# A dense layer's odd chunk of 96 hidden units, made with 128 columns of weights, on one Trainium2 core

## The chip, the cores and the metric

The kernel runs on one core of one Trainium2 chip. The metric is the device time of one execution in microseconds (us); of the kernel before there are three runs, and their median is used. TensorE (PE) multiplies a stationary operand, loaded by a weight load (PEld in the profile), with a moving operand that streams past it; results go to PSUM. VectorE (DVE), ScalarE (ACT) and GpSimd (POOL) work on SBUF and PSUM beside it; SyncE (SP) issues most transfers. Each engine runs its own instructions in order and waits on semaphores for the others.

## The reference, cut to what matters

Two kinds of layer alternate: attention (A), dense (B), attention, dense. Both layers of a kind share their weights.

```python
def _B_ref(x, w1, w2):               # x 2048 x 512, w1 512 x 1376, w2 1376 x 512
    h = jnp.einsum('bsd,df->bsf', x, w1)
    h = jnp.maximum(h, zero)
    return jnp.einsum('bsf,fd->bsd', h, w2)

x = x + _A_ref(_layernorm(x), A_mem0, Wq, Wk, Wv, Wo, seg_len)
x = x + _B_ref(_layernorm(x), w1, w2)
x = x + _A_ref(...)
x = x + _B_ref(...)
```

`_A_ref` goes through the 2,048 tokens in 64 segments of 32. Each segment attends, with 32 heads of 128, to itself and to 8 memory rows, and the first 8 rows of its output are the next segment's memory, so the segments form a recurrence. The dense layer maps each token on its own: 512 values to 1,376 hidden units, ReLU, and back to 512. The order of the hidden units doesn't matter, so long as the columns of `w1` and the rows of `w2` agree.

## The kernel before

**Steps.** One loop runs over `k`. Step `k` holds segment `k` of the first attention layer and segment `k - 4` of the second, so that the two recurrences run beside each other; at the start and at the end only one of them is there (a "single" step: k = 1 to 3 and 64 to 67). A step makes queries and keys for half of the heads (`qk(0)`, line 575), scores and softmax for them, then `qk(1)`, `scores` (line 609) and `softmax` of the other half, then `transpose_p` (line 656), `weighted_v` (line 682), the output projection of the memory rows (line 617), the new memory (line 820) and values (lines 346, 765).

**The dense layer.** Step `k` also does the dense layer for the rows that were finished two steps earlier, `d = k - 2`: normally 64 rows (32 from each of the two chains), sometimes 32. `dense_h` makes the hidden units, transposed: a chunk of hidden units lies on the partitions of PSUM, the rows lie along the free axis. 1,376 is 10 times 128 and 96 more, so there are `NFC = 11` chunks, and `F_LAST = 96`. For each chunk four matmuls run, one for each 128 of the 512 inputs; the stationary operand is a block of `w1` (128 inputs by the chunk's units) and the moving one the 64 (or 32) rows. So every matmul of line 507 has a weight load of its own. The chunks are made in two pieces: chunks 8 to 10 first, then 0 to 7 (three pieces in the last call: 8 to 10, 0 to 3, 4 to 7). A piece has one PSUM tile `hp`, of a pool of two buffers (`ps_fill`) that other stages use too. ReLU takes a piece from PSUM to `hT` in SBUF: the full chunks of a piece in one ACT instruction (line 513), the chunk of 96 units in another (line 515); in the last call chunks 4 to 7 go through DVE (line 511). `dense_y` (line 528) multiplies `hT` with `w2`; for the chunk of 96 units it uses 96 partitions of both. In all there are 67 passes through the dense layer; the last one has its own second half at line 1057, which takes the chunks in the order 8, 9, 10, 0 to 7.

**Where `dense_h` stands in a step.** The order of PE, DVE, SP and POOL is the order of the program, with calls under `tc.high_priority` and the rest written out by hand in `step`. In a normal step all 44 matmuls of `dense_h` come after `qk(1)` and before the second `scores`. In every fourth step up to k = 37 (`split(k)`: k = 5, 9, ... 37) and only there, the piece of chunks 8 to 10 stands there alone, and the other piece comes after the scores. In a single step `dense_h` comes after the second softmax. ACT is the one engine whose order isn't written out: a planner sorts its instructions by priority and by when it reckons that they are ready.

**What DVE does next to it.** `scores` adds into a PSUM tile in which DVE has put the mask (line 601), one tile for each of the two layers; the copies of the keys (line 583) and the softmax (lines 625, 629, 641, 642, 646) are DVE's too, the exponential (line 631) and the copies of the queries (line 581) ACT's.

Of the kernel before, what the change touches and what calls it, by code (L numbers as in the profile page):

```python
# [10 lines left out]
ACTF = mybir.ActivationFunctionType  # L11
# [11 lines left out]
def kernel(  # L23
# [14 lines left out]
    nc = tc.nc  # L38
# [4 lines left out]
    Dff = B_w1.shape[1]  # L43
# [7 lines left out]
    NFC = (Dff + 127) // 128  # L51
    F_LAST = Dff - (NFC - 1) * 128
# [43 lines left out]
    def span(d):  # L96
        offs = ([0] if has0(d) else []) + [o for o, _ in slots_of.get(d, [])]
        return base(d) + min(offs), base(d) + max(offs) + 32
# [52 lines left out]
    w1_sb = const.tile([128, NC4, Dff], BF)  # L151
    w2_sb = const.tile([128, NFC, Dm], BF)
# [3 lines left out]
    def load_dense():  # L156
        nc.sync.dma_start(out=w1_sb[:], in_=B_w1.rearrange("(c p) f -> p c f", p=128))
        nc.sync.dma_start(out=w2_sb[:, 0:NFC - 1, :],
                          in_=B_w2[0:(NFC - 1) * 128, :].rearrange("(c p) d -> p c d", p=128))
        nc.sync.dma_start(out=w2_sb[0:F_LAST, NFC - 1, :], in_=B_w2[(NFC - 1) * 128:Dff, :])  # L160

    mhalf_t = const.tile([128, 1], F32)
    nc.vector.memset(mhalf_t[:], -0.5)
# [322 lines left out]

    def dense_h(d, parts=slice(None)):
        if not 0 <= d <= LAST:  # L490
            return
        lo, hi = span(d)
        n = hi - lo

        def cols(c4):
            return xnT_tiles[d + 2][:, c4, lo:hi]

        if not parts.start:
            hT_tiles[d] = wk.tile([128, NFC, 64], BF, tag="hT", bufs=1, name="hT")
        hT = hT_tiles[d]  # L500
        pieces = ((8, NFC), (0, 4), (4, 8)) if d == LAST - 1 else ((8, NFC), (0, 8))
        for f0, f1 in pieces[parts]:
            hp = ps_fill.tile([128, 8, 64], F32, tag="fill", name="hp")
            for fc in range(f0, f1):
                fs = 128 if fc < NFC - 1 else F_LAST
                for c4 in range(NC4):
                    nc.tensor.matmul(hp[0:fs, fc - f0, 0:n], lhsT=w1_sb[:, c4, fc * 128:fc * 128 + fs],  # L507
                                     rhs=cols(c4), start=(c4 == 0), stop=(c4 == NC4 - 1))
            nfull = min(f1, NFC - 1) - f0
            if (f0, f1) == (4, 8):  # L510
                nc.vector.tensor_scalar_max(out=hT[:, f0:f1, 0:n], in0=hp[:, 0:nfull, 0:n], scalar1=0.0)
            else:
                nc.scalar.activation(out=hT[:, f0:f0 + nfull, 0:n], in_=hp[:, 0:nfull, 0:n], func=ACTF.Relu)
            if f1 == NFC:
                nc.scalar.activation(out=hT[0:F_LAST, NFC - 1, 0:n], in_=hp[0:F_LAST, nfull, 0:n], func=ACTF.Relu)

    def dense_y(d, f0, f1, bank=1):
        if not 0 <= d <= LAST:
# [376 lines left out]
    def step(k):  # L895
# [30 lines left out]
        def probabilities():  # L926

            softmax(0, act, by_pe, ess)
            if not by_pe:
                turn_p()  # L930
            if k % 4 == 3 and has_x:
                inputs_T(n_x)
            if has0(k + 1):
                load_x(k + 1)
            if k == 1:
                load_dense()
# [3 lines left out]
        if single:  # L940
            block(k, part, mid)
        elif light:
            dense_h(k - 2, slice(0, 1))
            block(k, part, 16)
        else:
            dense_h(k - 2)
# [3 lines left out]
        if single:  # L950
            dense_h(k - 2, slice(0, 1) if k == LAST else slice(None))
            block(k, mid, H)
            if k == LAST:
                keep_busy(3)
        elif light:
            dense_h(k - 2, slice(1, None))
            block(k, 16, H)
        else:
            block(k, part, H)
# [56 lines left out]
    with tc.manual_schedule(engines={mybir.EngineType.PE, mybir.EngineType.DVE, mybir.EngineType.SP,  # L1016
# [25 lines left out]
        d = LAST - 1  # L1042
# [10 lines left out]
        for fc in order:  # L1053
            fs = 128 if fc < NFC - 1 else F_LAST
            for q in range(4):
                u, j = divmod(q, 2)
# [45 lines left out]
```

## Time and profile before

| what | value |
|---|---|
| device time, median of 3 runs | 1598.08 us (1596.8 to 1599.88) |
| the profiled execution: its own time / its span | 1596.61 us / 1594.8 us |
| PE busy | 1565.9 us (98%), 42,680 matmuls |
| weight loads busy | 1320.7 us (83%) |
| DVE / ACT / POOL busy | 1268.4 (80%) / 738.9 (46%) / 349.8 us (22%) |
| clock granted to TensorE | 1.0 |
| line 507, PE busy (64 and 32 rows, 128 and 96 units) | 102.2 us, 2,948 matmuls |
| ReLU of full chunks, line 513 | 134 instructions, 35.8 + 17.0 + 2.7 + 1.3 us |
| ReLU of the chunk of 96 units, line 515 | 67 instructions, 12.9 + 1.1 us |

A profile page lists busy time by engine, then a chain of work followed back from the last instruction to what released it, then groups of instructions. In a group's row, `out<-in` names the tiles, `128*96` is the size of the stationary operand (inputs by columns), `128x64` the moving one or the tile, `xN` the count; after the bar stand the busy time, the mean duration of one in ns, and the idle time of the engine ahead of them. Durations of matmuls and weight loads overlap: what a stream of them costs is the distance from one start to the next, and that is read from the chain (a piece of the chain has its start, its length and the number of instructions in it) or from the starts of single instructions in the trace. "PE busy" therefore doesn't show by itself how fast PE goes.

### The profile page before, as it was taken

The page shows a single profiled execution, that of the slowest core. Times are in us where ns is not written, and L with a number is a line of the kernel's source. Part 1 is how long each engine was busy: PE and PEld are TensorE (multiplying, and loading weights), DVE is VectorE, ACT ScalarE, POOL GpSimd, SP SyncE. Part 2 cuts the span into 40 slices and gives each one's busy share as a digit, 9 for nine tenths or more (in the row PEclk, how much of TensorE's full clock was granted, in tenths as well). Part 3 has the DMA queues.
Part 4 walks back from the last instruction along what each step waited for, and adds up shares of the span by engine and source line. Part 5 has one row for each costly group of instructions (what it writes and reads, how often), then busy time and mean ns, then how long its engine had stood idle before and what let it go on. Part 6 is the DMA issues. An engine that isn't in the chain of part 4 may idle for free.

```text
span 1594.8 us, 94682 instructions
## 1 busy us (share of the span) xinstructions
PE 1565.9 (98%) x42680; PEld 1320.7 (83%) x42680; DVE 1268.4 (80%) x3115; ACT 738.9 (46%) x1799; POOL 349.8 (22%) x670
## 2 busy tenths in 40 slices
PE   6999999999999999999999999999999999999998
PEld 4677888888898888889888888988888898898886
DVE  4578888888888888888888888888878888887866
ACT  3434444444544544454454545445454544545433
POOL 2012222222222222222222222222222222222110
PEclk9999999999999999999999999999999999999999
DMA  9733343343343534444334443343443333233332
GB/s 369 237 78 74 76 87 89 65 98 86 77 78 83 94 64 95 84 73 87 83 87 71 98 83 77 84 83 82 80 98 79 74 88 79 78 77 93 70 75 41
DMA packets 222564, 146.38 MB, mean 92 GB/s; under 512 B 124008, under 2 KB 216528, under 8 KB 222160
## 3 DMA queue, kind: packets, MB, share of 16 engines
q1 hardware_dynamic: 218992, 136.09, 37.6%
q8 instruction: 335, 5.49, 1.5%
q0 software_dynamic: 3072, 4.20, 1.1%
q14 instruction: 69, 0.57, 0.1%
q10 hardware_dynamic: 96, 0.03, 0.0%
HBM read 65.41 MB, written 45.35 MB: 69 GB/s over the span
## 4 chain that ended last, share of the span: by engine, by line
PE 96%; DMA 2%; DVE 1%; SPq 1%; issue 0%; ACT 0%; POOL 0%; POOLq 0%; ACTq 0%
PE qp L575 38%; PE wox L365 10%; PE wo L617 8%; PE vm L765 7%; PE v L346 7%; PE hp L507 6%; PE sp L528 5%; PE pv L682 4%; PE sp L609 4%; PE vp L306 3%; DMA Wv_sb<-in_A_Wv_dram 2%; PE tp L656 1%; PE xp L478 1%; PE wox L388 1%; SPq L134 0%; PE mt L820 0%
## 5 line engine op out<-in xcount | busy, mean ns | idle before, releaser
L581 ACT CAST QT<-qp 128x480 bf16<-128x480 f32 (+3 forms) x408 | 201.7, 494 | 392.3 <-PE qp L575 392.2
L575 PE MATMUL qp<-HT,Wq_sb 128*128 128x80 bf16 (+1 forms) x8704 | 370.2, 200 | 2.1 <-POOL HT L754 1.2
L575 PE MATMUL qp<-HT,Wk_sb 128*128 128x80 bf16 (+1 forms) x8704 | 369.2, 199 | 1.5 <-DMA Wk_sb<-in_A_Wk_dram 0.7
L575 PEld LDWEIGHTS <-Wq_sb 128*128 128x128 bf16 x8704 | 325.6, 100 | 33.8 <-issue 26.5
L575 PEld LDWEIGHTS <-Wk_sb 128*128 128x128 bf16 x8704 | 328.2, 100 | 2.3 <-DMA Wk_sb<-in_A_Wk_dram 1.2
L583 DVE CAST KT<-qp 128x480 bf16<-128x480 f32 (+3 forms) x408 | 231.4, 568 | 124.0 <-PE qp L575 118.1
L646 POOL TENSOR_TENSOR P_sb<-es,sm 128x320 bf16<-128x320 f32 x185 | 130.9, 721 | 751.7 <-ACT es L631 502.2
L365 PE MATMUL wox<-Wo_sb,OTx 128*64 128x256 bf16 x2880 | 173.6, 273 | 0.0
L625 DVE TENSOR_REDUCE mx<-sp 128x8 f32<-128x320 f32 x256 | 115.0, 487 | 73.6 <-PE sp L609 72.7
L365 PEld LDWEIGHTS <-OTx 128*64 128x64 bf16 x2880 | 150.2, 110 | 2.9
L631 ACT ACTIVATE es<-es 128x320 f32<-128x320 f32 x256 | 110.7, 469 | 58.2 <-DVE es L629 57.2
L765 PE MATMUL vm<-Wv_sb,HTm 128*32 128x512 bf16 x2176 | 136.4, 380 | 0.6 <-DVE HT L834 0.6
L641 DVE TENSOR_REDUCE sm<-es 128x8 f32<-128x320 f32 x256 | 118.3, 462 | 15.0 <-ACT es L631 4.7
L617 PE MATMUL wo<-Wo_sb,OTm 128*32 128x512 bf16 x2144 | 128.9, 380 | 0.2 <-issue 0.2
L346 PE MATMUL v<-Wv_sb,xnT 128*32 128x512 bf16 x2048 | 129.0, 378 | 0.0
L601 DVE CAST sp<-maskb 128x320 f32<-128x320 bf16 x256 | 118.4, 484 | 0.0
L629 DVE TENSOR_TENSOR es<-sp,mx 128x320 f32<-128x320 f32 x256 | 113.8, 483 | 1.5
L765 PEld LDWEIGHTS <-HTm 128*32 128x32 bf16 x2176 | 90.6, 96 | 27.4 <-issue 12.3
L528 PE MATMUL sp<-w_sb,hT 128*64 128x256 bf16 (+4 forms) x1452 | 104.1, 275 | 0.2 <-issue 0.2
L769 ACT CAST VmS<-vm 128x512 bf16<-128x512 f32 x134 | 78.6, 587 | 53.8 <-PE vm L765 53.8
L507 PE MATMUL hp<-xnT,w_sb 128*128 128x64 bf16 (+3 forms) x2948 | 102.2, 193 | 0.5 <-DVE xnT L436 0.4
L507 PEld LDWEIGHTS <-w_sb 128*128 128x128 bf16 (+1 forms) x2948 | 95.1, 101 | 1.3 <-issue 0.7
(124 smaller groups left out, 2028.8 us busy)
## 6 DMA issues: line engine op xcount, KB each, us to landing
Vs<-vd SPq DMA_DIRECT2D x96, 256.0 KB
vd<-vst SPq DMA_DIRECT2D x181, 128.0 KB
vmd<-VmS SPq DMA_DIRECT2D x134, 128.0 KB
Vs<-vmd SPq DMA_DIRECT2D x254, 32.0 KB
Vs<-vmd SPq DMA_DIRECT2D x60, 128.0 KB
Wq_sb<-in_A_Wq_dram SPq DMA_DIRECT2D x2, 2048.0 KB
Wk_sb<-in_A_Wk_dram SPq DMA_DIRECT2D x2, 2048.0 KB
Wv_sb<-in_A_Wv_dram SPq DMA_DIRECT2D x2, 2048.0 KB
```

Of the source, the lines that this page charges most:

```text
L346: nc.tensor.matmul(vp[32 * j:32 * j + 32, :], lhsT=tokens[:, c4, :], rhs=Wv_sb[:, c4, n * 512:(n + 1) * 512], start=(c4 == 0), stop=(c4 == ...
L365: nc.tensor.matmul(out[64 * j:64 * j + nr, 0:256], lhsT=lhsT, rhs=rhs[:, 256 * j:256 * j + 256], start=start, stop=stop, tile_position=(0, ...
L507: nc.tensor.matmul(hp[0:fs, fc - f0, 0:n], lhsT=w1_sb[:, c4, fc * 128:fc * 128 + fs], rhs=cols(c4), start=(c4 == 0), stop=(c4 == NC4 - 1))
L528: nc.tensor.matmul(sp_banks[bank][64 * j:64 * j + n, 0:w], lhsT=hT_tiles[d][0:fs, fc, 0:n], rhs=w2_flat[0:fs, fc * Dm + 256 * j:fc * Dm + ...
L575: nc.tensor.matmul(qp[:, hi, 0:ncol], lhsT=W_sb[:, c4, h * Dh:(h + 1) * Dh], rhs=HT[:, c4, a_lo:a_hi, :], start=(c4 == 0), stop=(c4 == NC4 ...
L581: nc.scalar.copy(out=dst[:, 0:nh, a_lo * L:a_hi * L], in_=qp[:, 0:nh, 0:ncol])
L583: nc.vector.tensor_copy(out=dst[:, 0:nh, a_lo * L:a_hi * L], in_=qp[:, 0:nh, 0:ncol])
L601: nc.vector.tensor_copy(out=sp_tiles[a], in_=maskb2)
L617: nc.tensor.matmul(wo[32 * j:32 * j + 32, :], lhsT=OTm[:, h, n, 2 * M * c:2 * M * c + 4 * M], rhs=Wo_sb[:, h, :], start=(h < 4), stop=(h > ...
L641: nc.vector.tensor_reduce(out=sm[:], in_=es[:], axis=AX.X, op=ALU.add)
L646: eng.tensor_tensor(out=P, in0=es[:], in1=sm[:].unsqueeze(2).to_broadcast([128, 8, L]), op=ALU.mult)
L765: nc.tensor.matmul(vp[32 * j:32 * j + 32, :], lhsT=HTm[:, c4, :], rhs=Wv_sb[:, c4, n * 512:(n + 1) * 512], start=(c4 == 0), stop=(c4 == NC ...
```

## The change

The 1,376 hidden units are cut in another way. Chunks 0 to 9 are now units 96 to 1,375, and chunk 10 is made from columns 0 to 127 of `w1`: units 0 to 95, which are its own, and 96 to 127, which chunk 0 has too. The stationary operand of chunk 10 is therefore 128 columns wide as all others are. Its result fills 128 partitions of `hp`, so that one ReLU takes chunks 8, 9 and 10 together, and all 128 partitions of `hT`. The rows of `w2` are loaded in the same order of units: rows 96 to 1,375 for chunks 0 to 9, rows 0 to 95 for chunk 10. `dense_y` and line 1057 stay as they are; they read 96 partitions of chunk 10, so the 32 units that are made twice are used once.

```diff
-                          in_=B_w2[0:(NFC - 1) * 128, :].rearrange("(c p) d -> p c d", p=128))
-        nc.sync.dma_start(out=w2_sb[0:F_LAST, NFC - 1, :], in_=B_w2[(NFC - 1) * 128:Dff, :])
+                          in_=B_w2[F_LAST:Dff, :].rearrange("(c p) d -> p c d", p=128))
+        nc.sync.dma_start(out=w2_sb[0:F_LAST, NFC - 1, :], in_=B_w2[0:F_LAST, :])
...
-                fs = 128 if fc < NFC - 1 else F_LAST
+                u = F_LAST + 128 * fc if fc < NFC - 1 else 0
                 for c4 in range(NC4):
-                    nc.tensor.matmul(hp[0:fs, fc - f0, 0:n], lhsT=w1_sb[:, c4, fc * 128:fc * 128 + fs],
+                    nc.tensor.matmul(hp[:, fc - f0, 0:n], lhsT=w1_sb[:, c4, u:u + 128],
                                      rhs=cols(c4), start=(c4 == 0), stop=(c4 == NC4 - 1))
-            nfull = min(f1, NFC - 1) - f0
             if (f0, f1) == (4, 8):
-                nc.vector.tensor_scalar_max(out=hT[:, f0:f1, 0:n], in0=hp[:, 0:nfull, 0:n], scalar1=0.0)
+                nc.vector.tensor_scalar_max(out=hT[:, f0:f1, 0:n], in0=hp[:, 0:f1 - f0, 0:n], scalar1=0.0)
             else:
-                nc.scalar.activation(out=hT[:, f0:f0 + nfull, 0:n], in_=hp[:, 0:nfull, 0:n], func=ACTF.Relu)
-            if f1 == NFC:
-                nc.scalar.activation(out=hT[0:F_LAST, NFC - 1, 0:n], in_=hp[0:F_LAST, nfull, 0:n], func=ACTF.Relu)
+                nc.scalar.activation(out=hT[:, f0:f1, 0:n], in_=hp[:, 0:f1 - f0, 0:n], func=ACTF.Relu)
```

## The prediction

> **What bounds the kernel now.** I read the page first for the engines and the chain, then the busy time by stretches of the span, then the groups of the dense layer kept apart by shape, then the chain in short windows around the dense layer, and last the chain's end.
>
> The page:
>
> ```profile
> PE 1565.9 (98%) x42680; PEld 1320.7 (83%) x42680; DVE 1268.4 (80%) x3115; ACT 738.9 (46%) x1799; POOL 349.8 (22%) x670
> ...
> PEclk9999999999999999999999999999999999999999
> ...
> PE 96%; DMA 2%; DVE 1%; SPq 1%; issue 0%; ACT 0%; POOL 0%; POOLq 0%; ACTq 0%
> ```
>
> The stretches (length, busy PE, PEld, DVE, ACT, POOL, clock):
>
> ```profile
> 115.00:800.00 685.00, 682.38 (x18675) 585.60 (x18675) 565.94 (x1384) 323.06 (x792) 157.21 (x297) 1.00 0.40 82
> 800.00:1500.00 700.00, 699.94 (x19020) 597.14 (x19018) 573.77 (x1395) 336.17 (x817) 160.57 (x300) 1.00 0.38 82
> ```
>
> The chain that ended last is 96% PE, at full clock, and in 1,385 us of steady steps PE has 2.7 us without a matmul in flight. So the kernel takes as long as PE's stream of matmuls: a stage costs its count times the distance from start to start, and ACT's 739 us count only where PE waits for one.
>
> The dense layer's first half, shapes apart:
>
> ```profile
> L507 PE MATMUL hp<-xnT,w_sb 128*128 128x64 bf16 x2440 | 91.5, 193 | 0.5 <-DVE xnT L436 0.4
> ...
> L507 PEld LDWEIGHTS <-w_sb 128*128 128x128 bf16 x2680 | 87.8, 98 | 1.3 <-issue 0.7
> ...
> L507 PE MATMUL hp<-xnT,w_sb 128*96 128x64 bf16 x244 | 21.0, 209 | 0.0
> ...
> L507 PEld LDWEIGHTS <-w_sb 128*96 128x96 bf16 x268 | 17.3, 125 | 0.0
> ...
> L513 ACT ACTIVATE hT<-hp 128x128 bf16<-128x128 f32 x61 | 17.0, 278 | 36.1 <-PE hp L507 36.1
> ...
> L515 ACT ACTIVATE hT<-hp 96x64 bf16<-96x64 f32 x61 | 12.9, 211 | 0.0
> ```
>
> The smaller weight load is the longer one, 125 ns for 96 columns against 98 ns for 128, and its matmul takes 209 ns against 193. The chain in three windows gives the distance between starts (a split step, a normal one, and one with 32 rows):
>
> ```profile
> 797.03 0.41 PE hp L507 x12
> ```
>
> ```profile
> 820.04 1.35 PE hp L507 x44
> ```
>
> ```profile
> 120.74 1.17 PE hp L507 x44
> ```
>
> 44 matmuls less 12 are 32 of full width in 1.35 - 0.41 = 0.94 us: 29.4 ns each. The 12 are 8 of these, 0.235 us, and the four of 96 columns have 0.175 us, 44 ns each. Read from the trace's single starts it is sharper: 45.0 ns after a matmul with 96 columns, always, and 29.3 ns on average (median 29) after one with 128, with 64 rows; 45.0 and 25.4 ns with 32 rows (1.17 us is 40 of the one and four of the other). At the change to another shape the difference is the same, 139 against 123 ns.
>
> **The change, part by part.**
>
> *Four wider weight loads per pass.* 244 matmuls with 64 rows lie in 61 passes, 24 with 32 rows in 6. If a load of chunk 10 goes as its neighbours do, a pass of 64 rows gains 4 x (45.0 - 29.3) = 0.063 us and one of 32 rows 4 x (45.0 - 25.4) = 0.078 us: 61 x 0.063 + 6 x 0.078 = 3.8 + 0.5 = 4.3 us. The extra 32 columns cost nothing: a matmul's distance doesn't hang on how many columns are in use, since the ones with 128 are the closer.
>
> The Trainium skill (TensorE: Matmul & The Clock Gate) has a rule for each side. Its section on LDWEIGHTS puts a load at columns / 1.2 ns, 107 ns for 128 columns and 80 for 96; as an estimate from that page, 268 loads would then lose 7.1 us where the distance followed them. The 98 against 125 ns contradict that here. Its section on Fast Weight Load says that the fast path is on when there are 128 weights in a type other than fp32, and the rows agree: by it the sum is the one above.
>
> *Does PE's gain reach the end?* In normal steps `dense_h` stands between the second `qk` and the second `scores`, and the softmax behind the scores waits for them (in the view of waits DVE waits for the scores 138 times, 72.7 us in all). From there to the transposes of line 656 PE's work and DVE's chain are nearly of one length: the matmul starts 0.164 us after DVE's last product, and 0.146 us in the steps where it visibly waits. A gain behind the scores would be lost there; this one is ahead of them and moves both. What the scores need, the last key copy and the mask, ends 0.75 and 0.35 us before they start.
>
> In the nine split steps the mask ends 0.13 us after the first score, and the second layer's scores start at 0.204; with 0.056 us from a DVE end to a matmul, they would start at 0.13 + 0.063 + 0.056 = 0.249, which takes back 0.045 us, 0.4 us in all. But in those steps line 656 waits some 0.18 us for the softmax, whose first reduction needs the first layer's scores alone, so I take this loss as covered, and 0.4 us as its bound.
>
> *At the ends.* In the single steps 64 to 66, where `dense_h` comes after the scores, line 656 starts over 0.55 us after DVE's product, so the gain counts. In step 67 PE waits for the softmax behind it: its 0.08 us are lost. In steps 2 and 3 up to 0.15 us may be.
>
> *ReLU.* 67 instructions of 211 or 184 ns go, and the first of each pass grows by 64 or 32 elements. 128x192 isn't in the trace: between 278 ns (128x128) and 385 ns (the 128x256 row of the same view), halfway, 331. Today's pair, overlapped, takes 0.385 us (starts 0.174 apart). The first ReLU already waits for all 12 matmuls: it starts 0.037 us after the last of chunk 10, and the second has no wait of its own. So the joined one starts earlier with PE, and ends some 0.05 us sooner still. In steady steps that hides: no PE row there waits for `hT`. It counts once, in the last pass, whose third piece waits for the first piece's buffer:
>
> ```profile
> 1588.11 0.59 PE hp L507 x12
> ...
> 1588.78 0.28 ACT hT L513
> 1589.06 0.12 ACT hT L515
> ...
> 1589.22 0.63 PE hp L507 x16
> ```
>
> There 0.385 - 0.331 = 0.05 us are gained beside PE's 0.063.
>
> *ACT's order.* The planner may sort ACT anew. Now it puts the big ReLU between the two exponentials in split steps k = 9 to 37, and the waits at line 656 beyond the usual 0.107 us add up to 2.1 us over the steps after 200 us. A better order could give that back; the ReLU ahead of both would cost about 0.14 us in each of 8 steps, 1.1 us. I take none, as the joined ReLU stands where the pair stood.
>
> *Loads of w2.* Same sizes, same queue, same order: nothing, from either side, since line 528 waits for no DMA.
>
> Sum: 4.3 - 0.08 + 0.05 - half of 0.15 = 4.2 us. Against the profiled execution, 1596.61 us (span 1594.8 and 1.8 around it), that is 1592.4; this one lies 1.5 us below the median of 1598.08, from which the same gain gives 1593.9. That is 0.26%; a measurement here tells about 0.2% (3.2 us) from no change.
>
> **Rivals.**
>
> *The gain is hidden (1597.7).* If every step's length were set by something beside PE, 0.063 us of PE work would only lengthen a wait; then only the tail's 0.1 and some early steps remain. For it: the 0.02 us of margin between PE and DVE at line 656. Against it: that margin lies behind the scores, and 2.7 us of idle PE in 1,385. With ACT's worse order and the split steps' bound together the gain is 4.2 - 0.4 - 1.1 = 2.7 us, 1595.4, already within 0.2%.
>
> *The new starts of the columns are slow (1637).* Chunks 0 to 9 now start 192 bytes further along each row of w1. If the fast distance needed a start at a multiple of 256 bytes, 2,680 loads would go at 45 ns: 61 x 40 x 15.7 + 6 x 40 x 19.6 ns = 43 us, less the 4.3. It decides from 1.6 ns per load on. Against it: the four input blocks lie 2,752 bytes apart (10 x 256 + 192), so today's starts already fall on all four such offsets, and each of the four positions shows a median of 29 ns.
>
> *The load goes with its columns (1602).* Were the four loads of chunk 10 slower in the measure of 128 to 96, their distance would be 60 ns instead of 45: 268 x 15 ns = 4.0 us lost. The 98 ns row on the same line speaks against it. The rule cited above for LDWEIGHTS would have it so.
>
> *ACT in a worse order (1600 and more).* If the planner put the joined ReLU or the big one ahead of work that line 656 hangs on in normal steps, 0.1 us in 51 steps would take 5 us. The exponentials there start 1.03 us after ACT is free, which speaks against it.
>
> **How the numbers follow.** The forecast as summed, within 1 us: 0.70. Hidden wholly or in part: 0.17. Worse order of ACT: 0.08. Slow starts: 0.03. Load by columns: 0.02. The likeliest gives 1593.9, with 1592 to 1596 as its own range by the two bounds and the spread of the runs. Reaching down to ACT's better order (1593.9 - 2.1, and some spread: 1591.2) and up past the hidden case (1598.4) leaves out less than 0.2. Faster by over 0.2%: 0.70, for the forecast; some of it may come out within 0.2% by spread, and some of the partly hidden cases above it. Within: 0.16. Slower: 0.14.
>
> **What would show it.** After: all 2,948 loads of line 507 as 128x128 at 98 ns; 44 matmuls in 1.29 us of the chain in a normal step and 12 in 0.35 in a split one; 67 fewer ACT instructions and a 128x192 ReLU near 331 ns; steps 0.063 us shorter, evenly. Wrong if the 44 stay at 1.35 us, if the waits at line 656 grow by what line 507 loses, or if loads with 128 columns show more than 98 ns.

## The result, and the profile after

The changed kernel takes 1593.49 us (median of 14 runs, 1591.68 to 1597.58) against 1598.18 us before (14 runs). The medians differ by 4.7 us. The ratio is 0.997, with a 95% interval from 0.9962 to 0.9978, so the gain lies between 3.5 and 6.1 us. The forecast was 1593.9 us and 4.2 us less.

The page of the changed kernel, by the same rows as before (its lines are numbered a little differently: the matmul of `dense_h` is now line 508, the scores 607, the transposes 654):

```profile
PE 1561.4 (98%) x42680; PEld 1317.0 (83%) x42680; DVE 1267.3 (80%) x3115; ACT 734.8 (46%) x1732; POOL 349.6 (22%) x670
...
PE 96%; DMA 2%; SPq 1%; DVE 1%; issue 0%; ACT 0%; POOL 0%; POOLq 0%
```

The stretches of steady steps (length, busy PE, PEld, DVE, ACT, POOL with their instructions, clock, DMA share, GB/s):

```profile
115.00:800.00 685.00, 682.33 (x18710) 585.94 (x18709) 567.11 (x1390) 323.54 (x766) 157.82 (x298) 1.00 0.40 83
800.00:1500.00 700.00, 699.74 (x19058) 597.51 (x19056) 574.48 (x1399) 333.58 (x785) 160.30 (x300) 1.00 0.38 83
```

PE is still the chain. The same 1,385 us now hold 37,768 matmuls where they held 37,695, with 2.9 us of idle time instead of 2.7: the stream has become denser.

The groups of the dense layer's first half, shapes apart:

```profile
L508 PEld LDWEIGHTS <-w_sb 128*128 128x128 bf16 x2948 | 90.8, 98 | 1.3 <-issue 0.6
L508 PE MATMUL hp<-xnT,w_sb 128*128 128x64 bf16 x2684 | 90.0, 193 | 0.4 <-DVE xnT L436 0.4
...
L513 ACT ACTIVATE hT<-hp 128x192 bf16<-128x192 f32 x61 | 20.2, 331 | 32.6 <-PE hp L508 32.6
...
L513 ACT ACTIVATE hT<-hp 128x96 bf16<-128x96 f32 x6 | 1.5, 252 | 5.0 <-PE hp L508 4.9
```

All 2,948 loads now take 95 to 100 ns, 98 on average, and the loads of 125 ns are gone. The joined ReLU takes 331 ns. The chain in a split step, in a normal one and in the one with 32 rows:

```profile
795.38 0.35 PE hp L508 x12
```

```profile
818.33 1.28 PE hp L508 x44
819.61 0.51 PE sp L607 x32
```

```profile
121.37 1.09 PE hp L508 x44
```

0.41, 1.35 and 1.17 us have become 0.35, 1.28 and 1.09. Over the whole execution, the distances from each matmul of this line to the next start add up to 93.89 us, where they were 98.28: 4.39 us less. From one step's output projection to the next step's, the median step is 0.064 us shorter.

The two profiled executions differ by only 3.0 us (spans of 1594.8 and 1591.8). At the output projection of step 5 the changed one is 1.1 us late; weights and first values are still arriving in the steps before. At that of step 66 it is 2.8 us early, so 3.9 us are gained in between. The first steps vary like that without any change: two executions of the changed kernel are 1.7 us apart at step 5. The waits ahead of the first transpose in steps 2 to 4 were 0.20, 0.40 and 1.21 us in the kernel before, 0.20, 0.20 and 0.20 in the changed one, and 0.20, 0.40 and 0.21 us in its other execution.

The end of the chain. Before, the first matmul of `dense_h` there started at 1588.11 us, and the last product 1.74 us later:

```profile
1589.85 1.35 PE sp L1057 x44
```

After:

```profile
1585.20 0.98 PE hp L508 x28
1586.17 0.01 issue
1586.18 0.63 PE hp L508 x16
1586.81 1.35 PE sp L1055 x44
```

From the one to the other it is now 1.61 us, 0.13 less, and ACT is no longer a piece of the chain here.

### The profile page after: what moved, and what is told of

The parts are those of the page before. It is cut to its first block, busy times and chain, and to the rows that moved or that the text cites. A ratio compares the mean times of both kernels' runs of the same rounds, so it can differ in the third digit from the quotient of the medians.

```text
span 1591.8 us, 94615 instructions
## 1 busy us (share of the span) xinstructions
PE 1561.4 (98%) x42680; PEld 1317.0 (83%) x42680; DVE 1267.3 (80%) x3115; ACT 734.8 (46%) x1732; POOL 349.6 (22%) x670
## 4 chain that ended last, share of the span: by engine, by line
PE 96%; DMA 2%; SPq 1%; DVE 1%; issue 0%; ACT 0%; POOL 0%; POOLq 0%
PE qp L573 38%; PE wox L365 10%; PE wo L615 8%; PE vm L763 7%; PE v L346 7%; PE hp L508 5%; PE sp L526 5%; PE pv L680 4%; PE sp L607 4%; PE vp L306 3%; DMA Wv_sb<-in_A_Wv_dram 2%; PE tp L654 1%; PE xp L478 1%; PE wox L388 1%; SPq L134 0%
## 5 line engine op out<-in xcount | busy, mean ns | idle before, releaser
L508 PE MATMUL hp<-xnT,w_sb 128*128 128x64 bf16 (+1 forms) x2948 | 97.9, 192 | 0.4 <-DVE xnT L436 0.4
L513 ACT ACTIVATE hT<-hp 128x192 bf16<-128x192 f32 (+3 forms) x134 | 60.1, 448 | 72.9 <-PE hp L508 72.7
```

Source lines behind the costliest of these rows:

```text
L508: nc.tensor.matmul(hp[:, fc - f0, 0:n], lhsT=w1_sb[:, c4, u:u + 128], rhs=cols(c4), start=(c4 == 0), stop=(c4 == NC4 - 1))
```

## Experiments

All times are medians, and every ratio is to the kernel before, run beside the experiment on the same chip. It took 1598.55 us beside the two ReLUs, 127 columns, 64 columns and the other start, 1598.56 us beside less work ahead of and behind the scores, and 1599.07 us beside 72 columns and the halved ReLU.

**The wider loads alone.** The changed kernel with ReLU split as it was:

```diff
-                nc.scalar.activation(out=hT[:, f0:f1, 0:n], in_=hp[:, 0:f1 - f0, 0:n], func=ACTF.Relu)
+                nfull = min(f1, NFC - 1) - f0
+                nc.scalar.activation(out=hT[:, f0:f0 + nfull, 0:n], in_=hp[:, 0:nfull, 0:n], func=ACTF.Relu)
+            if f1 == NFC:
+                nc.scalar.activation(out=hT[0:F_LAST, NFC - 1, 0:n], in_=hp[0:F_LAST, nfull, 0:n], func=ACTF.Relu)
```

> Chunk 10 is made with 128 columns as in the change, but ReLU stays split as before: one instruction for chunks 8 and 9, one for the 96 partitions of chunk 10. If the gain comes from the closer matmuls alone: 1593.5 us against 1598.2 before, since all that is missing is the 0.05 us of the last pass; 44 matmuls of line 508 in 1.28 us of the chain. If the joined ReLU brings a share (67 instructions of ACT fewer), the time lies in between: half the share would be 1595.8.

Measured: 1594.06 us, ratio 0.9973 (0.9961 to 0.9984). The chain has the same 1.28 us for 44 matmuls, and ACT's busy time is back at 738.5 us. The median step is 0.066 us shorter than before, as with the change (0.064). So the wider loads bring the gain. The joined ReLU's share is within what the times can tell: without half of the gain this run would have come to 1596.2 us, just outside its interval, which ends at 1596.0.

**127 columns.** ReLU split as above, and chunk 10 one column narrower:

```diff
-                    nc.tensor.matmul(hp[:, fc - f0, 0:n], lhsT=w1_sb[:, c4, u:u + 128],
+                    w = 128 if fc < NFC - 1 else 127
+                    nc.tensor.matmul(hp[0:w, fc - f0, 0:n], lhsT=w1_sb[:, c4, u:u + w],
```

> Chunk 10 is made with 127 columns and ReLU split as before. If 128 columns are a special case and narrower loads go by their columns: 45 x 127 / 96 = 60 ns from start to start, 268 x 14.5 ns = 3.9 us slower than before, 1602.1 us. If any load that is nearly full goes at 29 ns, it is as fast as the change, 1593.5. If all narrower loads cost 45 ns whatever their width, 1598.2.

Measured: 1602.49 us, ratio 1.0023 (1.0014 to 1.0031), so slower than before. The groups, and the chain in a normal step:

```profile
L509 PEld LDWEIGHTS <-w_sb 128*128 128x128 bf16 x2680 | 88.6, 99 | 1.3 <-issue 0.7
L509 PEld LDWEIGHTS <-w_sb 128*127 128x127 bf16 x268 | 21.1, 139 | 0.0
```

```profile
820.82 1.40 PE hp L509 x44
```

One column less than 128 makes the load 139 ns long and the distance between matmuls 59 ns (median of 201), twice the 29 ns of 128 columns. The first expectation holds: the rival "the load goes with its columns" is true of 96 and 127 columns, and 128 columns are the exception.

**64 columns.** The same edit with 64; ReLU, `dense_y` and the last pass take 64 partitions of chunk 10.

```diff
+                    w = 128 if fc < NFC - 1 else 64
...
-            fs = 128 if fc < NFC - 1 else F_LAST
+            fs = 128 if fc < NFC - 1 else 64
```

> Chunk 10 is made with 64 columns, and 32 hidden units are left out of the result (dense_y and the last pass read 64 partitions of it). If narrower loads go by their columns: 64 / 96 x 45 = 30 ns, the same distance as with 128 columns, so 1593.7 us. If all narrower loads cost 45 ns: 1598.2.

Measured: 1611.59 us, ratio 1.008 (1.0067 to 1.0094). Neither expectation holds. The groups and the chain of a normal step:

```profile
L509 PEld LDWEIGHTS <-w_sb 128*64 128x64 bf16 x268 | 13.4, 110 | 3.3
...
L530 PE MATMUL sp<-w_sb,hT 64*64 64x256 bf16 x120 | 17.8, 293 | 0.0
```

```profile
824.37 1.51 PE hp L509 x44
```

Among themselves the narrow matmuls are close, 39 ns on average. But the first of them starts 122 ns after its neighbour with 128 columns, and the next one with 128 columns 127 ns after the last of them, where these distances were 29 and 45 ns. In `dense_y`, where chunk 10 now has 64 rows, the same happens. The distances of line 509 add up to 8.9 us more than before and those of `dense_y` to 6.6 us more; 13.0 us reached the end. My reading was that the array changes between a division for 128 columns and one for 64. The Trainium skill (TensorEngine Tiling (Array Packing), Key Properties) says that changing the tiling mode drains the engine, and gives no price. The next run tests whether narrow operands as such are slow or the change is.

**72 columns.** The same edit with 72.

> Chunk 10 is made with 72 columns, ReLU split as before, and 24 hidden units are left out of the result. 96 columns had 45 ns from start to start and 127 had 59, 0.46 ns a column; by that line 72 columns have 34 ns, 268 x 11 = 2.9 us less than before, 1595.6 us. If the 64 columns were slow because narrow loads as such are slow: 8 us or more above before, 1606. If they were slow because the matmuls around them had to change the array's division (123 and 128 ns at each change from 128 columns to 64 and back, where the others have 29 and 45), 72 columns show no such distances.

Measured: 1596.11 us, ratio 0.9982 (0.9972 to 0.9992): 3.0 us less than before.

```profile
L509 PEld LDWEIGHTS <-w_sb 128*72 128x72 bf16 x268 | 14.7, 118 | 0.0
```

```profile
820.47 1.31 PE hp L509 x44
```

The distance behind a matmul with 72 columns is 35 ns on all 201 occasions, and the one ahead of the first of them 29 ns (25 with 32 rows): no distance above 100 ns at the change of width. So 72, 96 and 127 columns have 35, 45 and 59 ns, about 0.44 ns for each column; 128 have 29. With 32 rows the three distances are the same 35, 45 and 59 ns, so the rows that stream past don't set them. An operand with fewer columns also fills fewer partitions of the result, and no run parts the two; that the load is what takes the time is the likelier reading (it is recorded as 118, 125 and 139 ns long), not a shown one.

A narrow operand as such is therefore not what made 64 columns dear; the cost lies at the two changes between 128 and 64. The split steps of that run agree: there chunk 10 is followed by values whose stationary operands have 64 columns too (line 306), and the next matmul starts 32 ns after the last of chunk 10, where it was 139 ns behind 96 columns. That what changes is a division of the array stays a reading; no view shows it.

**Another start.** As the change, but chunks 0 to 9 begin one column earlier, at 190 bytes past a step of 256 in the first input block, and the rows of `w2` are loaded to match:

```diff
-                u = F_LAST + 128 * fc if fc < NFC - 1 else 0
+                u = F_LAST - 1 + 128 * fc if fc < NFC - 1 else 0
```

> As the change, but chunks 0 to 9 start one column earlier, at 95 + 128 f, so that every weight load of theirs starts 190 bytes into a step of 256 (unit 95 counts twice and unit 1375 is left out of the result). If the start of the columns doesn't matter: 1593.5 us and 29 ns between starts. If a load needs a start at a multiple of 4 bytes or more for its fast distance: up to 43 us more, 1636.

Measured: 1594.56 us, ratio 0.9974 (0.9965 to 0.9984), with 1.28 us for 44 matmuls and a median of 29 ns between starts. A start that is only a multiple of 2 bytes into a row of `w1` costs nothing. The rival of the slow starts is gone; the changed kernel's own 29 ns had already spoken against it.

**Less work ahead of the scores.**

```diff
-                for c4 in range(NC4):
+                nc4 = NC4 if fc < 9 else 2
+                for c4 in range(nc4):
...
```

> As the change, but chunks 9 and 10 of the first half use two of the four input blocks (their sums are therefore incomplete): 4 matmuls fewer in each pass, ahead of the second scores in normal steps. 61 x 4 x 29.3 + 6 x 4 x 25.4 ns = 7.8 us, less some tenths in steps 2, 3 and 67. If PE's time ahead of the scores reaches the end in full: 1593.5 - 7.5 = 1586.0 us. If softmax or transfers already take over: well above, 1590 or more.

Measured: 1586.94 us, ratio 0.9934 (0.992 to 0.9947), 6.6 us under the changed kernel's median, some 2 us either way. The distances of line 509 fell by 7.7 us. The median step is 0.120 us shorter than in the changed kernel, where 4 x 29.3 ns = 0.117 us of matmuls went, so in a normal step a further cut ahead of the scores, almost twice the one of the change, still counts in full. Neither softmax nor a transfer had taken over.

**Less work behind the scores.**

```diff
         for fc in range(NFC)[f0:f1]:
+            if fc == 8:
+                continue
```

> As the change, but dense_y leaves chunk 8 out (its share is missing in the result): 2 matmuls fewer in each step, 0.107 us, which in normal steps stand between the second scores and the transposes. If PE and DVE are balanced there to 0.02 us, a normal step gains 0.02 us, the steps 64 to 66 the full 0.107: 1.1 us in all, 1592.4, and the distance to the first transpose grows to some 0.19 us. If the kernel were PE's stream alone, 66 x 0.107 = 7.1 us: 1586.4.

Measured: 1594.76 us, ratio 0.9976 (0.9966 to 0.9986): nothing gained on the changed kernel. In normal steps the distance from the last matmul of `dense_y` to the first transpose is 0.196 us where it was 0.107, so 0.089 of the 0.107 us turned into a wait. The view of waits shows it, first for the changed kernel and then for this one (weight loads of the transposes: us in total, times, longest):

```profile
PEld L654 <- issue: 3.3, 15, 0.4
```

```profile
PEld L656 <- issue: 11.4, 57, 0.4
```

15 waits have become 57. The 1.1 us that were expected to remain are below what the times can tell. In the trace they aren't there either: the first transpose comes 0.02 us sooner after `dense_y` begins (0.990 us instead of 1.009), but the transposes then take 0.276 us from the first to the last instead of 0.256, and the median step is as long as the changed kernel's (23.32 us in both). So a normal step gained nothing from this.

**The big ReLU in halves**, in the split steps only:

```diff
+                step_ = 4 if split(d + 2) and (f0, f1) == (0, 8) else f1 - f0
+                for g0 in range(f0, f1, step_):
+                    nc.scalar.activation(out=hT[:, g0:g0 + step_, 0:n], ...)
```

> As the change, but in the nine split steps the ReLU of chunks 0 to 7 is two instructions of four chunks, so that only one of them stands between the two exponentials. If that ReLU is what the first transpose waits for in steps 9 to 37, its distance falls from 224 ns towards 107: at most 8 x 0.117 = 0.9 us less than the change, 0.06%, under what the times can tell; if the wait hangs on something else, the 224 ns stay.

> The changed kernel itself, beside the two others: 1593.5 us, and half_relu within 1 us of it.

Measured: 1593.01 us, ratio 0.9966 (0.9954 to 0.9979), beside the changed kernel with 1594.6 us, ratio 0.9976 (0.9966 to 0.9986). The medians are 1.6 us apart, where at most 1 was expected, but the two intervals overlap, so the times don't part them. The chain does, at the transposes of one split step, in the changed kernel's second execution and in this one:

```profile
800.37 0.42 PE tp L654 x16
```

```profile
801.44 0.30 PE tp L657 x16
```

The distance to the first transpose fell from about 217 to 107 ns in all eight steps 9 to 37. In the trace, seven of these eight steps are 0.12 us shorter than in the changed kernel; the eighth is 0.08 us longer, which this experiment doesn't explain. The ReLU between the exponentials was what these steps waited for.

## Why the prediction was right

*The widths.* The step that carried the forecast was the price of four wider loads, 4 x 15.7 ns in a pass of 64 rows. It measured out: 4.39 us in all on line 508 against 4.3, with no column of the added 32 costing anything. The Trainium skill's rule on Fast Weight Load (TensorE: Matmul & The Clock Gate) asks for 128 weights in a type other than fp32. The step from 127 to 128 columns, 59 to 29 ns, agrees. The Trainium skill's rule of columns / 1.2 ns (the same page, LDWEIGHTS) has the right sense from 72 to 127 columns; as an estimate from it a column is worth 0.83 ns, where the distances here grow by 0.44.

*It reaches the end.* Normal steps became 0.064 us shorter, where 0.063 was said. The reason given, that the gain lies ahead of the scores and moves softmax along, was only argued; the pair of experiments shows it. Ahead of the scores 6.6 of 7.5 forecast us arrived. Behind them 0.089 us of 0.107 became a wait at the first transpose, as the 0.02 us margin read from the trace of before would have it, and the transposes behind took the rest back.

*Split steps.* The second layer's scores start 0.245 us after the first, as said (0.249, before 0.204), and the wait at the first transpose covered it: it shrank from 0.285 to 0.224 us, and these steps gained the full amount.

*The ends.* The last pass gained 0.13 us where 0.063 + 0.05 was reckoned. The terms for the early steps and for step 67 can't be checked: the first steps vary by more than the 0.15 us in question, and the last ones by more than the 0.08. That the total came within half a microsecond of the forecast is in part luck: the interval of the gain is 2.6 us wide, and single steps of the two profiled executions differ by up to 0.7 us.

*ReLU and ACT's order.* 331 and 252 ns (331 for 128x192 forecast). Except that the pair is one instruction, the order of all ACT's instructions is the one of before, so the cases with a better or worse order didn't occur. Splitting the big ReLU shows that the waits in split steps, 8 x 0.11 us, are indeed ACT's; the change leaves them. That is less than half of the 2.1 us of waits at the transposes that the prediction counted in all steps after 200 us; what the others wait for stays open.

*The rivals.* The hidden gain is refuted by the shorter steps and by the cut ahead of the scores, the slow starts by the start at column 95. Loads that go by their columns exist, but not at 128.

## What to carry to other kernels

Where PE's stream is the bound, read the distance from matmul to matmul for each width of the stationary operand: an odd remainder of 96 columns can cost half as much again as a full 128, so filling it up with columns that something else has already, and ignoring the surplus rows, pays. The gain counts in full only where PE's time still decides: ahead of the work that the next wait hangs on, not behind it. Don't shrink a remainder to 64 columns among full ones without looking at the distances at each change of width.

## What the runs showed that was not expected

A stationary operand of 64 columns between others of 128 costs 122 and 127 ns at the two changes, 8.9 us on line 509, while 72 columns are free of it and go at 35 ns. The 8.9 us are counted against the 96 columns of before. The loads' own durations in the groups' rows, 110 ns for 64 and 118 for 72, say nothing of this: only the distances from start to start do.
